# The second batch of a fused attention and FFN kernel takes the order of work of the later batches

## The chip, the cores and the metric

The kernel runs on one core of one Trainium2 chip. The metric is the device time of one execution in microseconds (us): the kernel before takes 320.41 us (median of 3 runs, 319.65 to 321.46). A change counts as faster or slower from 2% on.

Engines are named as in the profile: PE is TensorE (matrix products), PEld its weight loads, DVE VectorE, ACT ScalarE, POOL GpSimd and SP SyncE. A matrix product writes to PSUM, and ACT or DVE read it from there; SBUF is the working memory.

## The reference

Eight batches of attention with eight heads, 576 positions and head dimension 64, with a relative-position bias; then a feed-forward layer (FFN) on the 4608 x 512 result, whose hidden value is the largest of three products.

```python
scores = (1.0 / np.sqrt(D)) * np.matmul(q, k.transpose(0, 1, 3, 2))     # (8, 8, 576, 576)
scores = scores + bias.transpose(2, 0, 1)[None]       # bias_table[bucket(|i - j|)], one table per head
scores = scores - np.max(scores, axis=-1, keepdims=True)
attn = np.exp(scores)
attn = attn / (np.sum(attn, axis=-1, keepdims=True) + 1e-09)
attn_out = np.matmul(attn, v)
x = attn_out.transpose(0, 2, 1, 3).reshape(B * S, H * D)                # 4608 x 512
h = np.maximum(np.maximum(x @ w1, x @ w2), x @ w3)                       # 4608 x 768
out = h @ w_out                                                          # 4608 x 512
```

## The kernel before

The kernel works on pairs of heads: `(b, hp)` is pair `hp` (0 to 3) of batch `b` (0 to 7), so "batch two" is `b == 1`. Scores are made transposed, keys on the partitions. 576 is four tiles of 128 and 64 left over. A pair is done in two halves. Each half has a *visit*, which makes the scores of 256 queries against the 512 main keys: two `sc` tiles in PSUM, four matmuls each, and one exponential each on ACT. The left-over keys give `sct` (one exponential of 576), the left-over queries give `scq` (512 elements in all). DVE multiplies the exponentials with the bias (`times_band`, tile by tile in `t`). One pair later `attend` multiplies them with V into a tile `a`, in two halves, and `quotients` (a reciprocal and a product on DVE) divides by the sums into `x_sb`.

```python
ps_s = ctx.enter_context(tc.tile_pool(name="ps_s", bufs=2, space=bass.MemoryType.PSUM))   # tag "sc": 2 banks each
ps_a = ctx.enter_context(tc.tile_pool(name="ps_a", bufs=2, space=bass.MemoryType.PSUM))   # tag "a"
ps_f = ctx.enter_context(tc.tile_pool(name="ps_f", bufs=2, space=bass.MemoryType.PSUM))   # tag "ff"
...
def visit(qT, kT, e4, c, mid=None, el=None):
    if el is not None:                     # left-over scores inside the visit
        banks = [ps_a.tile([P, KT * 64], F32, tag="a", name="scq") for _ in range(2)]
        turn_left_queries(qT, kT, banks)
        put_left_queries(el, banks)        # two exponentials of 256
    for tt in range(0, KT, 2):
        sc = ps_s.tile([P, 2, 2, QS], F32, tag="sc", name="sc")
        ...                                # four matmuls
        exp(e4[:, tt : tt + 2, :, c * QS : c * QS + QS].rearrange("p t h q -> p h t q"), sc[:])
...
def left_queries(hp, qT, kT, el):          # left-over scores outside the visit
    sc = ps_s.tile([P, 2, CH], F32, tag="sc", name="scq")
    turn_left_queries(qT, kT, [sc[:, par, 0 : KT * 64] for par in range(2)])
    ...                                    # one exponential of 512
...
def second_transposes(made, hp):           # batch two's q and k of a pair are turned by PE
    tp = ps_s.tile([P, 2, 2 * CH], BF16, tag="sc", name="tp")
    ...                                    # ten transposes; dve_copy to qT, act_copy to kT, a main part and a tail each
```

The FFN of earlier tokens fills the gaps of the attention. It is cut into blocks: `f`, `m`, `g` are the products with `w1`, `w2`, `w3`, each worth 4 matmuls of 512 columns (8 of 256 where the chunk has 256 tokens); `o` is an output block of 6. A list of portions holds them, and `fill(rate, *hooks)` takes portions while their sum stays within `rate`. The hooks are the attention's work that stands among the blocks: all of them come before the last block, or earlier if there are more of them than blocks left.

```python
def fill(target, *hooks):
    groups, spent, hooks = [], 0, list(hooks)
    while pending and (not groups or spent + pending[0][0] <= target):
        n, fns = pending.pop(0)
        spent += n
        groups += [fn for fn in fns if fn]
    for j, group in enumerate(groups):
        while hooks and (j == len(groups) - 1 or j > 0 and len(hooks) > len(groups) - 1 - j):
            hooks.pop(0)()
        group()
    for hook in hooks:
        hook()
```

The loop over the pairs, with cuts:

```python
for b, hp in [(b, hp) for b in range(1, B) for hp in range(HP)]:
    ...
    together = b > 1 and (b, hp) != (2, 0)
    rate = 8 if b == 1 or (b, hp) == (2, 0) else 13
    visit(qT, kT, e4, 0)
    ...                                    # a transpose of x_sb of batch 0, where one is left
    quotients = next_late()                # attend of the pair before, first half
    times_band(hp, e4, 0, 0, QS, inorder)
    quotients()
    if b == 1 and hp + 1 < HP:
        spread_packed(hp + 1, nc.vector)   # the next pair's q and k, two copies on DVE
    ...
    def keys():
        left_keys(hp, qT, kT, el, 0, S)    # sct
        if together:
            next_late()()                  # attend of the pair before, second half, and its quotients
    fill(rate, keys, *([lambda: None] if together else []))
    times_bandt(hp, el)

    visit(qT, kT, e4, 1, el=el if together else None)
    ...
    if not together:
        quotients = next_late()            # attend of the pair before, second half
        times_band(hp, e4, 1, 0, QM, inorder)
        quotients()
    if b == 1 and hp + 1 < HP:
        second_transposes(qk[1], hp + 1)
    ...
    fill(rate, bands_2, queries)           # queries: left_queries if not together
    times_band_left(hp, el)
    for half in range(2):
        late.append(lambda b=b, hp=hp, e4=e4, el=el, half=half: attend(b, hp, e4, el, half))
```

Every tag of a PSUM pool is a ring of two: a new tile waits until the tile two before it has been read. The matmuls, the DVE operations of the attention and the copies of the turned q and k keep the order of the program on their engines.

Of the kernel before, what the change touches and what calls it, by code (L numbers as in the profile page):

```python
# [39 lines left out]
def kernel(  # L40
# [19 lines left out]
    HP = H // 2  # L60
    QS = 2 * P
    QM = 2 * QS
# [28 lines left out]
    inorder = tc.keep_in_program_order  # L91
# [4 lines left out]
    def tr(*args):  # L96
        inorder(nc.tensor.transpose(*args))
# [219 lines left out]
    def ffn(t0, nt, last):  # L317
# [77 lines left out]
        f, m, g = ([(DCH, lambda fn=fn, fb=fb: fn(fb)) for fb in range(n_fb)] for fn in (first, second, third))  # L395
        o = [(FCH, lambda j=j: output(j)) for j in range(nt // P)]
        if per == 1:
            portions = [[f[0], m[0]]]
            for fb in range(1, n_fb):
                portions.append([g[fb - 1], f[fb], m[fb]])  # L400
            portions.append([g[-1], (0, None), o[0]])
        else:
            if not t0:
                portions = [[f[0]], [m[0], f[1]], [m[1]], [f[2], m[2]]]
                deferred.append(([[g[0]], g[1:]], [[x] for x in o]))
                o = []
            else:
                portions = [x for gs, _ in deferred for x in gs]
                for fb in range(n_fb):
                    portions += [[f[fb], m[fb]], [g[fb]]]  # L410
                portions += [x for _, os in deferred for x in os] + [[o[0]]]
                o = o[1:]
        if len(o) > 2:
# [3 lines left out]
    pending, rest, stores, deferred, idle_sums = [], [], [], [], []  # L417
# [21 lines left out]
# [13 lines that stand above are left out]
# [55 lines left out]
    def second_transposes(made, hp):  # L507

        hs = slice(2 * hp, 2 * hp + 2)
        tp = ps_s.tile([P, 2, 2 * CH], BF16, tag="sc", name="tp")  # L510
        for j, tl in enumerate((qtail, ktail)):
            for t in range(KT):
                tr(tp[:, j, P * t : P * t + P], batch[1][j][:, t, hs, :].rearrange("p h d -> p (h d)"), ident[:])
            tr(tp[:, j, KT * P : KT * P + P], tl[1][:, hp, :], ident[:])
        main = [
            copy(
                made[j][:, hp, 0 : KT * P].rearrange("c (p t) -> c p t", t=KT),
                tp[:, j, 0 : KT * P].rearrange("c (t p) -> c p t", t=KT),
            )
            for j, copy in enumerate((dve_copy, act_copy))  # L520
        ]
        tail = [
            copy(made[j][:, hp, KT * P :], tp[:, j, KT * P : n])
            for j, (copy, n) in enumerate(((dve_copy, S), (act_copy, (KT + 1) * P)))
        ]
        other_banks([main[1], tail[1]], [main[0], tail[0]])
        other_banks([tail[0]], [main[1]])

    def times_band(hp, e4, t, lo, hi, put=lambda x: x):
        lo, hi = max(lo, P * t - P), min(hi, P * t + 2 * P)  # L530
        if lo < hi:
            c0, c1 = BAND - (hi - P * t + P), BAND - (lo - P * t + P)
            put(nc.vector.tensor_tensor(  # L533
                out=e4[:, t, :, lo:hi], in0=e4[:, t, :, lo:hi],
                in1=hank[:, 2 * hp : 2 * hp + 2, c0:c1][:, :, ::-1], op=ALU.mult,
            ))
# [17 lines left out]
    def visit(qT, kT, e4, c, mid=None, el=None):  # L554

        if el is not None:
            banks = [ps_a.tile([P, KT * 64], F32, tag="a", name="scq") for _ in range(2)]
            turn_left_queries(qT, kT, banks)
            put_left_queries(el, banks)
        for tt in range(0, KT, 2):  # L560
            sc = ps_s.tile([P, 2, 2, QS], F32, tag="sc", name="sc")
            for t in range(2):
                for par in range(2):
                    r = slice(64 * par, 64 * par + 64)
                    mm(
                        sc[:, par, t, :], lhsT=kT[r, P * (tt + t) : P * (tt + t) + P],
                        rhs=qT[r, c * QS : c * QS + QS],
                    )
            exp(e4[:, tt : tt + 2, :, c * QS : c * QS + QS].rearrange("p t h q -> p h t q"), sc[:])
            if tt == 0 and mid:  # L570
                mid()
# [17 lines left out]
    def left_queries(hp, qT, kT, el):  # L589

        sc = ps_s.tile([P, 2, CH], F32, tag="sc", name="scq")
        turn_left_queries(qT, kT, [sc[:, par, 0 : KT * 64] for par in range(2)])
        eq = el[:, S:].rearrange("p (t h q) -> p h t q", t=KT, h=2)
        exp(eq, sc[:, :, 0 : KT * 64].rearrange("p h (t q) -> p h t q", t=KT))
# [75 lines left out]
    def next_late():  # L670
        return late.pop(0)() if late else (lambda: None)
# [9 lines left out]
    qk = [qk_tiles(), qk_tiles()]  # L681
# [45 lines left out]
    for hp in range(HP):  # L727
        qT, kT = (x[:, hp, :] for x in qk[0])
        e4, el = e_tiles()
# [28 lines left out]
    for hp in range(HP):  # L758
        qT, kT = (x[:, hp, :] for x in qk[0])
        e4, el = e_tiles()  # L760
# [20 lines left out]
        quotients = next_late()  # L781
        if hp < 2:
# [5 lines left out]
            quotients = next_late()  # L788
# [24 lines left out]
    for b, hp in [(b, hp) for b in range(1, B) for hp in range(HP)]:  # L813
        if hp == 0:
            x_sb[b] = x_tile()
        qT, kT = (x[:, hp, :] for x in qk[b])
        e4, el = e_tiles()
        together = b > 1 and (b, hp) != (2, 0)
        rate = 8 if b == 1 or (b, hp) == (2, 0) else 13

        visit(qT, kT, e4, 0)
        store_outputs()
        if b == 1:
            if hp == 0:
                crossbar = transposes(2)
            next(crossbar, None)
        elif hp and b + 1 < B:
            if hp == 1:  # L830
                crossbar = transposes(b + 1)
            next(crossbar)
        early()
        if turned:
            turned.pop(0)()
        quotients = next_late()
# [3 lines that stand above are left out]
            spread_packed(hp + 1, nc.vector)  # L840
        if (b, hp) == (1, 1):
            add_ffn(QS, QS)

        def keys():
            left_keys(hp, qT, kT, el, 0, S)
            if together:
                next_late()()

        fill(rate, keys, *([lambda: None] if together else []))
        times_bandt(hp, el)  # L850


        visit(qT, kT, e4, 1, el=el if together else None)
        store_outputs()
        if b == 1 or hp in (1, 2) and b + 1 < B:
            next(crossbar, None)
        early()
        if turned:
            turned.pop(0)()
        if not together:  # L860
            quotients = next_late()
            times_band(hp, e4, 1, 0, QM, inorder)
            quotients()
        if b == 1 and hp + 1 < HP:
            second_transposes(qk[1], hp + 1)
        if hp == 1 and b > 1:
            add_ffn((b - 1) * CH, CH)
        if hp == (2, 2, 0)[min(b, 3) - 1] and b + 1 < B:
            if b == 1:
                load_last_weights(turned_qk[2, 1, 1])  # L870
            load_v(b + 1, 0, H, turned_qk[b + 1, 1, KT - 1] if b < 3 else None)
        if (b, hp) == (2, 0):
            batch[3] = load_tiles()
            load_qk(3, divided[1, HP - 1, 1])
        if hp == 2 and 1 < b < B - 2:
            batch[b + 2] = load_tiles()
            load_qk(b + 2, turned_qk[b + 1, 1, KT - 1])

        def queries():
            if not together:  # L880
                left_queries(hp, qT, kT, el)
            times_band(hp, e4, 3, 0, QM, inorder)

        def bands_2():
            for t in range(1 if together else 2, 3):
                times_band(hp, e4, t, 0, QM, inorder)

        if together:
            idle_sums.append(hp)
        fill(rate, bands_2, queries)  # L890
        idle_sums.clear()
        times_band_left(hp, el)
        for half in range(2):
            late.append(lambda b=b, hp=hp, e4=e4, el=el, half=half: attend(b, hp, e4, el, half))
# [44 lines left out]
```

The softmax here doesn't subtract the row's maximum and nothing guards it: scores larger than these inputs give would overflow.

## Time and profile before

| | busy us | share of the span | instructions |
|---|---|---|---|
| PE | 307.0 | 96% | 3328 |
| DVE | 214.0 | 67% | 535 |
| ACT | 201.3 | 63% | 297 |
| POOL | 108.0 | 34% | 143 |

The span of the profiled execution is 319.7 us, and the granted PE clock is full after the first quarter of the slices. A busy share is a mean over stages with different work, so the stage in question has to be looked at by itself: pairs (1, 0) to (2, 1) lie between 36.2 and 77.1 us of the span. In a timeline, the first number is the start of an instruction (or of a run of equal ones) and the second its length, both in us; the number in brackets is how long its engine had been idle before, and what ended that. Instructions of one engine may overlap a little.

### The profile page before, as it was taken

The page shows a single profiled execution, that of the slowest core. Times are in us where ns is not written, and L with a number is a line of the kernel's source. Part 1 is how long each engine was busy: PE and PEld are TensorE (multiplying, and loading weights), DVE is VectorE, ACT ScalarE, POOL GpSimd, SP SyncE. Part 2 cuts the span into 40 slices and gives each one's busy share as a digit, 9 for nine tenths or more (in the row PEclk, how much of TensorE's full clock was granted, in tenths as well). Part 3 has the DMA queues.
Part 4 walks back from the last instruction along what each step waited for, and adds up shares of the span by engine and source line. Part 5 has one row for each costly group of instructions (what it writes and reads, how often), then busy time and mean ns, then how long its engine had stood idle before and what let it go on. Part 6 is the DMA issues. An engine that isn't in the chain of part 4 may idle for free.

```text
span 319.7 us, 8238 instructions
## 1 busy us (share of the span) xinstructions
PE 307.0 (96%) x3328; PEld 172.1 (54%) x3328; DVE 214.0 (67%) x535; ACT 201.3 (63%) x297; POOL 108.0 (34%) x143
## 2 busy tenths in 40 slices
PE   7768899999999999999999999999999999999995
PEld 2346677775555555555555555555555554444442
DVE  7476678786676666666777667777677675554552
ACT  4958898886677677776777677667776751121221
POOL 8848831349059430852087029500000000000000
PEclk9969999999999999999999999999999999999999
DMA  9999999999999999999999999994042103301103
GB/s 166 198 196 198 180 150 126 135 114 133 206 157 138 127 203 163 84 127 178 190 96 145 163 196 130 157 195 108 2 77 98 36 2 74 133 0 69 64 0 131
DMA packets 163878, 40.34 MB, mean 126 GB/s; under 512 B 153720, under 2 KB 159360, under 8 KB 163840
## 3 DMA queue, kind: packets, MB, share of 16 engines
q0 software_dynamic: 103776, 16.66, 78.0%
q1 hardware_dynamic: 58304, 22.69, 39.1%
q10 hardware_dynamic: 1760, 0.47, 0.6%
q8 instruction: 26, 0.43, 0.6%
q14 instruction: 12, 0.10, 0.1%
HBM read 35.39 MB, written 9.45 MB: 140 GB/s over the span
## 4 chain that ended last, share of the span: by engine, by line
PE 74%; DMA 1%; ACT 1%; issue 0%
PE ps L94 40%; PE pso L94 13%; PE a L94 11%; PE sc L94 7%; PE sct L94 2%; PE scq L94 2%; DMA out_dram<-osb 1%; ACT e L539 0%; ACT osb L388 0%; ACT osb L107 0%
## 5 line engine op out<-in xcount | busy, mean ns | idle before, releaser
L94 PE MATMUL ps<-xT,w_bf 128*128 128x512 bf16 (+1 forms) x720 | 152.2, 358 | 0.6 <-ACT xT L107 0.6
L539 ACT ACTIVATE e<-sc 128x1024 bf16<-128x1024 f32 x128 | 124.5, 1031 | 20.5 <-PE sc L94 17.9
L94 PEld LDWEIGHTS <-w_bf 128*128 128x128 bf16 x720 | 65.4, 98 | 63.4 <-issue 5.8
L533 DVE TENSOR_TENSOR e<-e,hank 128x512 bf16<-128x512 bf16 (+2 forms) x136 | 58.5, 466 | 11.3 <-ACT e L539 9.4
L345 ACT ACTIVATE m<-ps 128x512 bf16<-128x512 f32 x48 | 29.3, 609 | 51.9 <-PE ps L94 51.9
L354 DVE TENSOR_TENSOR m<-ps,m 128x512 bf16<-128x512 f32 x48 | 33.0, 688 | 34.2 <-PE ps L94 34.0
L94 PEld LDWEIGHTS <-kT 64*128 64x128 bf16 (+1 forms) x832 | 30.0, 95 | 38.2 <-issue 25.1
L94 PE MATMUL pso<-wo_bf,hT 128*128 128x512 bf16 (+2 forms) x222 | 50.3, 373 | 0.0
L94 PE MATMUL a<-vx,e 128*128 128x65 bf16 x1024 | 46.4, 195 | 0.0
L360 DVE TENSOR_TENSOR hT<-ps,m 128x512 bf16<-128x512 f32 x48 | 33.0, 688 | 15.9 <-PE ps L94 14.5
L94 PE MATMUL sc<-qT,kT 64*128 64x256 bf16 x512 | 41.0, 273 | 2.8 <-ACT e L539 1.3
L94 PEld LDWEIGHTS <-e 128*128 128x128 bf16 x1024 | 42.1, 99 | 0.8
L139 POOL DMA_DIRECT2D vx<-in_v_dram x32 | 28.5, 911 | 28.8 <-PE scq L94 12.6
L167 POOL DMA_DIRECT2D q_sb<-in_q_dram x24 | 22.0, 918 | 46.2 <-DMA qT<-qtail 26.3
L94 PE MATMUL a<-vt,el 128*128 128x130 bf16 x160 | 36.0, 225 | 0.8 <-DMA vt<-in_v_dram 0.8
L110 DVE COPY osb<-pso 128x512 f32<-128x512 f32 (+1 forms) x33 | 22.6, 686 | 18.0 <-PE pso L94 14.7
L641 DVE TENSOR_TENSOR x_sb<-a,rd 128x256 bf16<-128x256 f32 (+1 forms) x64 | 31.4, 490 | 2.2
L539 ACT ACTIVATE el<-scq 128x256 bf16<-128x256 f32 (+1 forms) x55 | 20.5, 416 | 19.4 <-PE scq L94 19.2
L94 PEld LDWEIGHTS <-hT 128*128 128x128 bf16 x222 | 20.1, 97 | 22.4 <-issue 1.5
L94 PEld LDWEIGHTS <-el 128*128 128x128 bf16 x416 | 24.3, 97 | 10.2 <-issue 5.7
L539 ACT ACTIVATE el<-sct 128x576 bf16<-128x576 f32 (+2 forms) x36 | 21.8, 607 | 5.8 <-PE sct L94 4.5
L167 POOL DMA_DIRECT2D k_sb<-in_k_dram x24 | 22.1, 920 | 1.3 <-DMA w_bf<-in_moe_w_dram 1.2
(71 smaller groups left out, 168.6 us busy)
## 6 DMA issues: line engine op xcount, KB each, us to landing
out_dram<-osb SPq DMA_DIRECT2D x35, 256.0 KB, 3.5
vx<-in_v_dram POOLq DMA_DIRECT2D x32, 128.0 KB, 8.3
q_sb<-in_q_dram POOLq DMA_DIRECT2D x26, 128.0 KB, 5.8
k_sb<-in_k_dram POOLq DMA_DIRECT2D x24, 128.0 KB, 6.7
w_bf<-in_moe_w_dram POOLq DMA_DIRECT2D x3, 768.0 KB, 9.8
xT<-in_k_dram SPq DMA_DIRECT2D x6, 128.0 KB, 4.9
hank<-w_dr SPq DMA_DIRECT2D x2, 384.0 KB, 6.7
wo_bf<-in_moe_w_out_dram POOLq DMA_DIRECT2D x1, 768.0 KB, 7.9
```

Source lines behind the costliest of these rows:

```text
L94: inorder(nc.tensor.matmul(*args, **kw))
L110: return inorder(nc.vector.tensor_copy(out_, in_))
L139: in_turn(b, nc.gpsimd.dma_start(out=dst[:, t, h0:h1, :], in_=x[:, t, h0:h1, :])) for t in range(t0, t1)
L167: loads.append(in_turn(b, nc.gpsimd.dma_start(out=dst[:, t], in_=main_part(src, b)[:, t])))
L345: nc.scalar.activation(out=st[fb]["m0"][:], in_=ps0, func=ACTF.Copy)
L354: inorder(nc.vector.tensor_tensor(out=m[:], in0=ps1, in1=st[fb]["m0"][:], op=ALU.max))
L360: inorder(nc.vector.tensor_tensor(out=block(fb), in0=ps2, in1=other, op=ALU.max))
L533: put(nc.vector.tensor_tensor(out=e4[:, t, :, lo:hi], in0=e4[:, t, :, lo:hi], in1=hank[:, 2 * hp : 2 * hp + 2, c0:c1][:, :, ::-1], op=ALU. ...
L539: nc.scalar.activation(out=out_, in_=in_, func=ACTF.Exp, scale=inv_sqrt_d)
L641: divided[b, hp, half] = inorder(nc.vector.tensor_tensor(out=x_sb[b][:, 2 * half : 2 * half + n, P * hp : P * hp + P].rearrange("p t (h d) ...
```

## The change

Pairs (1, 0) to (2, 0) take the order of work that all later pairs have already. The left-over queries' scores go into the second visit (tag "a" and not "sc", two exponentials and not one), the second half of the pair before is attended in the first half, behind the left-over keys, and its quotients follow at once. The turning of the next pair's q and k, which stood ahead of the second half's FFN, becomes a hook there: behind the first of two blocks, and behind the bands of `t` 1 and 2. The FFN portions of batch 0's second chunk are cut so that a first half gets one block and a second half two, where it was the other way round. Pair (2, 1) gets rate 8 in its first half. It is meant to have the exponentials follow each other more closely, with less waiting for tiles of the tag "sc", and to spread the work more evenly over the halves.

```diff
@@ in ffn(): portions of the second chunk of batch 0
                 for fb in range(n_fb):
-                    portions += [[f[fb], m[fb]], [g[fb]]]
+                    portions += [[f[fb]], [m[fb], g[fb]]]
@@ in the loop over the pairs
-        together = b > 1 and (b, hp) != (2, 0)
         rate = 8 if b == 1 or (b, hp) == (2, 0) else 13
...
         def keys():
             left_keys(hp, qT, kT, el, 0, S)
-            if together:
-                next_late()()
-
-        fill(rate, keys, *([lambda: None] if together else []))
+            next_late()()
+
+        fill(8 if (b, hp) == (2, 1) else rate, keys, lambda: None)
         times_bandt(hp, el)
...
-        visit(qT, kT, e4, 1, el=el if together else None)
+        visit(qT, kT, e4, 1, el=el)
...
-        if not together:
-            quotients = next_late()
-            times_band(hp, e4, 1, 0, QM, inorder)
-            quotients()
-        if b == 1 and hp + 1 < HP:
-            second_transposes(qk[1], hp + 1)
...
         def queries():
-            if not together:
-                left_queries(hp, qT, kT, el)
             times_band(hp, e4, 3, 0, QM, inorder)
 
         def bands_2():
-            for t in range(1 if together else 2, 3):
+            for t in range(1, 3):
                 times_band(hp, e4, t, 0, QM, inorder)
 
-        if together:
-            idle_sums.append(hp)
-        fill(rate, bands_2, queries)
+        idle_sums.append(hp)
+        turn = [lambda: second_transposes(qk[1], hp + 1)] if b == 1 and hp + 1 < HP else []
+        fill(rate, bands_2, *turn, queries)
         idle_sums.clear()
```

`idle_sums` lets the product `f` of a second half write to a tile of the tag "a" instead of "ff".

## The prediction

> **What bounds the kernel now.** I read the page first, then busy time by stretches of 8 us, then the chain of waits, then the timelines of PE, ACT and DVE between 36 and 79 us. The stretches first (columns: stretch; then for PE, PEld, DVE, ACT and POOL busy us and number of instructions; clock; DMA share; GB/s):
>
> ```profile
> 48.00:56.00 8.00, 8.00 (x134) 6.39 (x131) 6.53 (x18) 6.49 (x10) 0.84 (x1) 1.00 1.35 126
> 56.00:64.00 8.00, 7.80 (x123) 6.01 (x120) 6.34 (x18) 7.19 (x11) 2.72 (x4) 1.00 1.06 135
> 64.00:72.00 8.00, 8.00 (x126) 5.96 (x126) 6.46 (x18) 6.94 (x10) 3.76 (x5) 1.00 1.33 113
> ...
> 88.00:96.00 8.00, 8.00 (x95) 4.42 (x94) 5.85 (x14) 5.88 (x9) 4.18 (x6) 1.00 1.06 156
> ```
>
> From about 78 us on PE is the bound: 8.00 of 8 busy, and the chain of waits holds PE pieces end to end. There a second half's scores and its pair's other products cost (starts in the PE timeline) 0.54 for eight `sc`, 0.60 for 18 `a`, 0.24 for `sct`, 0.90 for 27 `a`, 0.13 for eight `scq`, 0.54 for eight `sc`: 2.95 us a pair, and a block of four 512-column products takes 0.86, or 0.216 a unit.
>
> In the changed stretch PE reads as just as busy, but its matmul ends are modelled, and ACT is at 6.5 to 7.2 of 8 and DVE at 6.3 to 6.5: three engines near full, each waiting for the others in turn. So I count PE's need against the clock. Six pairs (1, 0) to (2, 1): 6 x 2.95 = 17.7; FFN units 5 x 12 + 18 = 78, x 0.216 = 16.8; three turnings of ten transposes, 0.56 each = 1.7; three `x_sb` transposes, 0.17 each = 0.5. Sum 36.7. The first `sc` of (1, 0) starts at 36.20 and the first `a` of (2, 2) at 78.21; without waits that `a` would come at 36.20 + 36.7 + 0.53 = 73.4. So PE loses 4.8 us here, 1.5% of the kernel. No work leaves the kernel, and by the start of (2, 2) both orders have done the same 78 units; so 4.8 us is the most that can be gained, and a gain over 2% is as good as excluded.
>
> PE around the last turning:
>
> ```profile
> 55.83 0.38 PE L97 MATMUL tp<-ident,q_sb 128*128 128x128 bf16 x4
> 56.05 0.22 PE L97 MATMUL tp<-ident,qtail 128*128 128x128 bf16 x1
> 56.11 0.39 PE L97 MATMUL tp<-ident,k_sb 128*128 128x128 bf16 x4
> 56.33 0.22 PE L97 MATMUL tp<-ident,ktail 128*128 128x128 bf16 x1
> 56.74 0.29 PE L94 MATMUL scq<-qT,kT 64*128 64x64 bf16 x8 [0.20 <-ACT e L539]
> 56.97 1.05 PE L94 MATMUL ps<-xT,w_bf 128*128 128x256 bf16 x8
> 57.95 0.61 PE L94 MATMUL sc<-qT,kT 64*128 64x256 bf16 x8
> ```
>
> and ACT there and in the next two pairs:
>
> ```profile
> 54.76 1.94 ACT L539 ACTIVATE e<-sc 128x1024 bf16<-128x1024 f32 x2 [0.22 <-PE sc L94]
> 56.59 0.77 ACT L107 ACTIVATE kT<-tp 128x512 bf16<-128x512 bf16 x2
> 57.23 0.61 ACT L539 ACTIVATE el<-scq 128x512 bf16<-128x512 f32 x1
> 58.43 1.94 ACT L539 ACTIVATE e<-sc 128x1024 bf16<-128x1024 f32 x2 [0.59 <-ACT el L539]
> ...
> 69.49 0.60 ACT L539 ACTIVATE el<-scq 128x512 bf16<-128x512 f32 x1
> 70.51 1.94 ACT L539 ACTIVATE e<-sc 128x1024 bf16<-128x1024 f32 x2 [0.42 <-ACT el L539]
> 72.92 0.65 ACT L539 ACTIVATE el<-sct 128x576 bf16<-128x576 f32 x1 [0.47 <-PE sct L94]
> 75.34 0.66 ACT L539 ACTIVATE el<-scq 128x256 bf16<-128x256 f32 x2 [1.76 <-PE scq L94]
> 75.88 3.78 ACT L539 ACTIVATE e<-sc 128x1024 bf16<-128x1024 f32 x4
> ```
>
> The reader should see two kinds of hole on ACT: 0.4 to 0.6 us behind each `scq` exponential, because the next visit's `sc` comes a short `sc` ring later, and 1.76 us in (2, 1), where twelve FFN units stand before `scq`; behind that ACT runs four exponentials without a pause and PE waits for it. These are what the change aims at. And DVE at that turning:
>
> ```profile
> 55.81 0.56 DVE L533 TENSOR_TENSOR e<-e,hank 128x768 bf16<-128x768 bf16 x1 [0.46 <-ACT e L539]
> 56.29 0.19 DVE L640 RECIPROCAL rd<-a 128x6 f32<-128x6 f32 x1
> 56.51 0.56 DVE L641 TENSOR_TENSOR x_sb<-a,rd 128x384 bf16<-128x384 f32 x1
> 56.98 0.78 DVE L110 COPY qT<-tp 128x512 bf16<-128x512 bf16 x2
> 57.68 0.88 DVE L533 TENSOR_TENSOR e<-e,hank 128x768 bf16<-128x768 bf16 x2
> ```
>
> Here the copy to qT comes before the bands that need the second visit's last exponential, and it is done at 57.76, just before the next visit at 57.95.
>
> **What the Trainium skill says.** "ScalarE: Activation LUTs", section "What ACT_TABLE_LOAD costs", gives 186 ns plus 0.833 ns per element for an activation with immediate scale and bias, and an overlap of some 93 ns between two. That is 1039 ns for 1024 and 612 for 512; the trace has 1024 to 1031 and 601. Two of 256 are 2 x 399 - 93, an estimate of 0.71 us; the trace has 0.66 (75.34 above). "TensorE: Matmul & The Clock Gate", section "The mechanism" under packing, says that matmuls start and end in program order; the trace agrees: no `scq` passes an FFN block. "PSUM — Partial Sum Buffer", "Specifications (TRN2)", counts 8 banks of 2 KiB: the three pools take 4 + 2 + 2, so the waits on rings can't be eased by another bank. No view of the trace shows the banks; the sizes in the code do.
>
> **The change part by part.** One pair in the new order, from its first `sc` at 0, in us.
>
> First half, no turning ((1, 3)): the first exponential starts at 0.49 (43.77 to 44.26 in the trace), the second ends at 2.4. PE: `sc` to 0.54, 18 `a` to 1.14, `sct` to 1.38, 27 `a` to 2.28, one block to 3.15. `scq` takes the two tiles of tag "a" that the two attends had, so it waits for the later quotients: reciprocal 0.2 after the last `a` (73.62 to 73.82), 0.79 for reciprocal and product (73.82 to 74.61), so 3.3 us. One block covers 0.87 of that 1.0. ACT: `sct` exponential, the block's copy from 3.4 to 3.9, `scq` to 4.4, then two exponentials to 6.3. PE has its two blocks behind the second visit and reaches the next pair at 5.7; that pair's second `sc` waits for 6.3. So about 5.8 for (1, 3) and 6.0 for (2, 0), against 6.04 each (57.95, 63.99, 70.03). Gain 0.2. The second `scq` exponential adds only 0.06 and lies in ACT's chain.
>
> Pair (2, 1): six units instead of twelve stand before `scq`; the 1.29 us of one output block still cover the quotients. PE needs 2.95 + 3.9 = 6.85 and loses only the start of the second `sc`. I expect the next pair's first `a` 7.7 to 7.8 after its start instead of 8.18. Gain 0.45.
>
> Pairs with a turning ((1, 0), (1, 1), (1, 2)), here (1, 2): two copies of the packed q and k stand on DVE between the two quotients (53.52 to 54.01 in the trace), so `scq` starts at 3.65 and not 3.3. The second visit ends on PE at 4.3, the first block at 5.2. `tp` takes the first `sc`'s tile, whose exponential ends at 5.5: `tp` 5.55 to 6.1, last block to 7.0. On DVE the copy to qT now stands behind the bands of `t` 1 and 2. Band 2 needs the last exponential, which ends at 6.45: band 2 starts at 6.55, 0.48 each, copy main part 0.68 (the 128x512 form), so qT is there at 7.7, and the next `sc` starts at 7.75 instead of 7.0. Before, this pair took 6.87: a loss of 0.9. For (1, 1) the same 7.75 against 7.31: 0.45. For (1, 0), whose first half gets a longer DVE queue (one copy took 0.65) and two more ACT copies, I get 44.5 for the end against 43.77: 0.75. Sum 2.1 lost.
>
> Net: +2.1 - 0.2 - 0.45 = +1.45 us on 320.41, which is 321.9. I take 0.3 off for the rival that I hold likeliest: 321.6.
>
> **The rivals.** First, the gain that was meant: the turning's copies do not matter, because ACT and PE queue enough work. Then the loss of 4.8 us falls to perhaps 3, the three turning pairs take about 6.9 each (21.8 before, 7.57 + 7.31 + 6.87, so 1.1 less), and the sum with the other gains is 318.7. For it speaks that ACT is nearest its limit in these pairs and that the holes of 0.4 to 0.6 are removed; against it, that qT has so little margin already (0.19) and now stands behind one more wait. Second, the wait for the quotients takes the place of the wait on "sc": if DVE is later than I have it, each of six pairs loses 0.3 more, 323.4. For it, DVE is at 6.3 to 6.5 of 8; against, between exponential and quotients I count free time in the first half. Third, nothing: transfers or the later stretch swallow it. In later stretches PE is busy throughout, so a shift in the start of (2, 2) should move the end by just as much; a null would need gains and losses that cancel, 320.4, which is well within reach here.
>
> **Range and chances.** Range 319.2 to 323.2: the lower end is near the first rival, the upper near the second. The bound of 1.5% rules out a faster verdict, and 2% slower would need 6.4 us more, as if all of today's waits came a second time and more. Chances: faster 0.01, same 0.97, slower 0.02.
>
> **What would show it.** Right: in the timeline of the changed kernel the qT copy of the three turnings starts behind a band that waits for ACT's exponential, and the next visit's `sc` starts 0.05 to 0.2 after it, with ACT idle for about 1 us between the kT copy and the next exponential; `scq` starts within 0.1 of the end of an `x_sb` product of 384; pairs (1, 3) and (2, 0) last 5.7 to 6.1; the 1.76 us hole in (2, 1) shrinks, and PE no longer waits in the first visit of (2, 2). From the first `a` of (2, 2) on, both traces should run in parallel. Wrong: turning pairs of 7 us or less, or a qT copy ahead of the bands, would give the first rival; a difference that arises only after 80 us would mean that I looked in the wrong stretch.

## The result and the profile after

| | before | changed | ratio, 95% interval |
|---|---|---|---|
| first comparison | 320.07 us (4 runs) | 323.74 us (4 runs) | 1.0109 [1.0075, 1.0143] |
| second, later | 321.10 us (40 runs) | 323.10 us (21 runs) | 1.0053 [1.0034, 1.0071] |

The changed kernel is slower by 0.5 to 1%, "same" by the 2% rule but clear of noise. 321.6 was predicted, with 323.2 as the upper end; the first comparison lies above it.

The busy time by stretches in the changed kernel (columns as before):

```profile
48.00:56.00 8.00, 7.02 (x108) 5.35 (x106) 6.56 (x19) 5.63 (x9) 0.84 (x1) 1.00 1.23 132
56.00:64.00 8.00, 6.80 (x106) 5.32 (x105) 5.34 (x16) 6.12 (x10) 4.76 (x6) 1.00 1.48 140
64.00:72.00 8.00, 7.84 (x121) 6.10 (x121) 4.67 (x14) 7.07 (x12) 1.35 (x2) 1.00 0.89 68
...
88.00:96.00 8.00, 7.95 (x94) 4.40 (x94) 5.55 (x15) 5.83 (x10) 1.62 (x2) 1.00 0.76 188
```

PE was 8.00, 7.80 and 8.00 in the first three; now it has visible holes, and ACT fell from 6.49 and 7.19 to 5.63 and 6.12 in the first two. From 56 to 64 us PE, ACT and DVE all do less than before, so no engine has become a new bound; the stretches only suggest a longer chain of dependences, and the timelines have to show it. Around the turning behind (1, 2), the counterpart of the one shown of before, PE:

```profile
58.25 0.38 PE L97 MATMUL tp<-ident,q_sb 128*128 128x128 bf16 x4 [0.44 <-ACT e L539]
58.47 0.22 PE L97 MATMUL tp<-ident,qtail 128*128 128x128 bf16 x1
58.53 0.39 PE L97 MATMUL tp<-ident,k_sb 128*128 128x128 bf16 x4
58.75 0.22 PE L97 MATMUL tp<-ident,ktail 128*128 128x128 bf16 x1
58.81 1.04 PE L94 MATMUL ps<-xT,w_bf 128*128 128x256 bf16 x8
60.36 0.61 PE L94 MATMUL sc<-qT,kT 64*128 64x256 bf16 x8 [0.52 <-DVE qT L110]
...
61.92 0.41 PE L94 MATMUL sct<-qT,kT 128*128 128x512 bf16 x2 [0.24 <-ACT e L539]
```

ACT:

```profile
57.16 1.96 ACT L539 ACTIVATE e<-sc 128x1024 bf16<-128x1024 f32 x2
59.01 0.77 ACT L107 ACTIVATE kT<-tp 128x512 bf16<-128x512 bf16 x2
60.84 1.94 ACT L539 ACTIVATE e<-sc 128x1024 bf16<-128x1024 f32 x2 [1.06 <-issue]
62.67 0.66 ACT L539 ACTIVATE el<-sct 128x576 bf16<-128x576 f32 x1
64.13 0.60 ACT L342 ACTIVATE hT<-ps 128x512 bf16<-128x512 f32 x1 [0.81 <-PE ps L94]
```

DVE:

```profile
58.53 1.18 DVE L533 TENSOR_TENSOR e<-e,hank 128x768 bf16<-128x768 bf16 x2
59.62 0.78 DVE L110 COPY qT<-tp 128x512 bf16<-128x512 bf16 x2
60.32 0.41 DVE L533 TENSOR_TENSOR e<-e,hank 128x512 bf16<-128x512 bf16 x1
```

And the chain of waits there (start, length, what):

```profile
57.28 1.84 ACT e L539 x2
59.13 0.02 issue
59.15 0.04 DVE e L533
59.19 0.44 issue
59.62 0.16 DVE qT L110
59.79 1.06 issue
60.84 1.03 ACT e L539
61.88 0.04 issue
61.92 0.41 PE sct L94 x2
```

Read it as a path: the last exponential of a visit, the band that needs it, the copy to qT queued behind that band, the next visit, its first exponential, and then `sct`, which waits for that exponential. (In the kernel before, the chain as the profile follows it back ends at 76.91 us, so it can't be compared here; its timelines can.) `issue` of 1.06 us stands for the rest of the copy's main part (0.68 in all) and the four matmuls ahead of the exponential; the view doesn't name them.

Most comparisons below rest on one measure, the start of the first `sc` of a pair in the PE timeline. "Stage" is from that of (1, 0) to that of (2, 3). What lies ahead of it differs between executions of the same instructions: (1, 0) starts at 36.20 and 34.69 us in two traces of the kernel before, and in the others between 34.15 and 37.40. The stage is steadier: 50.23 and 50.22 in those two, 53.06 and 52.82 in two of the changed kernel. The 0.24 between the last two lies in (1, 0).

| us between first `sc` | (1, 0) | (1, 1) | (1, 2) | (1, 3) | (2, 0) | (2, 1) + (2, 2) | stage |
|---|---|---|---|---|---|---|---|
| before | 7.57 | 7.31 | 6.87 | 6.04 | 6.04 | 16.40 | 50.23 |
| before (second trace) | 7.57 | 7.31 | 6.86 | 6.05 | 6.04 | 16.39 | 50.22 |
| changed | 8.52 | 7.78 | 7.99 | 6.25 | 6.31 | 16.21 | 53.06 |
| changed (second trace) | 8.27 | 7.79 | 7.99 | 6.26 | 6.30 | 16.21 | 52.82 |
| turning first | 8.51 | 7.20 | 7.52 | 6.25 | 6.31 | 16.21 | 52.00 |
| attend first | 8.19 | 7.72 | 7.76 | 5.78 | 6.38 | 16.02 | 51.85 |
| both | 8.49 | 7.12 | 7.81 | 6.18 | 6.17 | 16.02 | 51.79 |
| before, rate 8 in (2, 1) | 7.58 | 7.31 | 6.86 | 6.04 | 6.04 | 16.21 | 50.04 |
| queries behind | 7.46 | 6.81 | 6.61 | 6.02 | 6.01 | 16.02 | 48.93 |
| queries behind, bands first | 7.47 | 7.34 | 7.19 | 6.02 | 6.01 | 16.02 | 50.05 |
| before, turning as hook | 7.57 | 7.56 | 7.20 | 6.04 | 6.04 | 16.39 | 50.80 |
| changed, old portions | 8.45 | 7.79 | 8.25 | 6.15 | 6.85 | 16.51 | 54.00 |
| queries last (second trace) | 7.58 | 6.58 | 6.64 | 6.08 | 6.08 | 15.97 | 48.93 |

In the changed order the length of (1, 0) hangs on a copy. DVE copies the packed q and k of the next pair between the two quotients, and `scq` waits for the second of these. One of the two copies, mostly 0.28 us long, took longer there: 0.74 us in the first trace of the changed kernel, 0.50 in the second, 0.74 in "turning first", 0.41 in "attend first", 0.70 in "both", 0.67 in "changed, old portions". In all six traces (1, 0) less this copy is 7.77 to 7.79 us. So differences of (1, 0) among these six come from the copy, and not from the edits; the last section says what the copy met.

### The profile page after: what moved, and what is told of

Same layout as the page of the kernel before. It is cut to its first block, busy times and chain, and to the rows that moved or that the text cites. A ratio compares the mean times of both kernels' runs of the same rounds, so it can differ in the third digit from the quotient of the medians.

```text
span 322.3 us, 8204 instructions
## 1 busy us (share of the span) xinstructions
PE 306.2 (95%) x3288; PEld 173.2 (54%) x3328; DVE 213.1 (66%) x535; ACT 201.2 (62%) x302; POOL 108.1 (34%) x143
## 4 chain that ended last, share of the span: by engine, by line
PE 79%; ACT 3%; issue 2%; DMA 1%; DVE 1%
PE ps L94 41%; PE pso L94 14%; PE a L94 13%; PE sc L94 7%; ACT e L539 2%; PE sct L94 2%; PE scq L94 2%; DMA out_dram<-osb 1%; DVE e L533 0%; DVE hT L360 0%; ACT kT L107 0%; ACT osb L388 0%; ACT hT L342 0%; ACT el L539 0%; ACT osb L107 0%
## 5 line engine op out<-in xcount | busy, mean ns | idle before, releaser
L94 PE MATMUL ps<-xT,w_bf 128*128 128x512 bf16 (+1 forms) x693 | 148.3, 357 | 2.0 <-ACT xT L107 0.6
L94 PE MATMUL pso<-wo_bf,hT 128*128 128x512 bf16 (+2 forms) x209 | 47.6, 373 | 0.7
```

Source lines behind the costliest of these rows:

```text
L94: inorder(nc.tensor.matmul(*args, **kw))
```

## The experiments

### The turning ahead of the bands

```diff
-        fill(rate, bands_2, *turn, queries)
+        fill(rate, *turn, bands_2, queries)
```

> The changed kernel, with the turning's hook ahead of the bands of t 1 and 2, so that DVE copies qT before it multiplies those bands. Theory A (the copy to qT stands behind a band that waits for the last exponential, and the next visit waits for it): the next visit's first sc comes 0.58 us earlier after (1, 1) and (1, 2), where PE would be done with its last block at 51.78 and 59.78 instead of starting at 52.37 and 60.36; nothing is gained after (1, 0), where the copy to kT on ACT sets the start (44.5). The later bands give back 0.1 to 0.2. Sum -1.0, 322.7 us. Theory B (the loss is in the waits of the first half, sct for the first exponential and scq for the quotients, and the turning is hidden by them): the time moves by less than 0.3 us, 323.5 or more.

Measured: 321.68 us beside 321.15 of before, ratio 1.0023 [0.9998, 1.0047]. The stage is 52.00, 1.06 less than changed: (1, 1) 0.58 and (1, 2) 0.47 shorter, (1, 0) unchanged, as theory A had it. The copy's place behind the bands is one cause, and about 1.1 of the 2.83 us.

### The second attend ahead of the left-over keys

```diff
-            left_keys(hp, qT, kT, el, 0, S)
             next_late()()
+            left_keys(hp, qT, kT, el, 0, S)
```

(It holds for the later batches too, where it changed nothing: (2, 2) takes 8.77 in both traces.)

> The changed kernel, with the second attend ahead of the left-over keys in the first half, so that sct, whose tile is the one of the first sc, is asked for 0.9 us later. Theory B: sct no longer waits 0.24 + 0.2 us for the first exponential; in (1, 3) the left-over queries come 0.4 us earlier, in (1, 1) and (1, 2) nothing is gained since DVE's two copies of packed q and k set the start of scq there, in (2, 0) little. Sum -0.5, 323.2 us, and no wait before sct in the PE timeline. Theory A: that wait is hidden by another one behind it, and the time stays at 323.7 within 0.2.

Measured: 322.12 beside 321.15, ratio 1.0022 [0.9996, 1.0048]; stage 51.85, 1.21 less than changed. No `sct` waits any more. PE in (1, 3):

```profile
62.88 0.41 PE L94 MATMUL a<-vx,el 128*128 128x65 bf16 x8
63.12 0.41 PE L94 MATMUL sct<-qT,kT 128*128 128x512 bf16 x2
63.37 1.04 PE L94 MATMUL ps<-xT,w_bf 128*128 128x256 bf16 x8
64.34 0.29 PE L94 MATMUL scq<-qT,kT 64*128 64x64 bf16 x8
64.46 0.60 PE L94 MATMUL sc<-qT,kT 64*128 64x256 bf16 x8
65.00 1.92 PE L94 MATMUL ps<-xT,w_bf 128*128 128x256 bf16 x16
66.85 0.39 PE L94 MATMUL sc<-qT,kT 64*128 64x256 bf16 x4
```

Everything follows without a wait: 5.78 us for the pair where the changed kernel takes 6.25, a gain of 0.47 for 0.4 expected. (2, 1) and (2, 2) gain 0.19 and (1, 2) gains 0.23. In (1, 2) I had DVE alone in the way; but ACT copies the FFN block's product ahead of the exponential of `scq`, and with `sct` no longer waiting, the block and this copy come 0.40 earlier (3.36 us into the pair and not 3.76), the exponential 0.29 and the turning 0.28 (5.60 and not 5.88). The 0.33 of (1, 0) is luck: the copy there took 0.41 us and not 0.74. Without it the gain is 0.88. Theory B holds as well.

### Both

> Both edits. If A and B each name a wait of its own, the gains add: -1.5, 322.2 us. If they are one chain, the sum is no better than the better of the two, 322.7.

Measured: 321.88 beside 321.15, ratio 1.0026 [1.0008, 1.0044]; stage 51.79, hardly less than with the better edit alone. In (1, 2), 7.81, PE has

```profile
53.77 0.20 PE L94 MATMUL scq<-qT,kT 64*128 64x64 bf16 x1
54.67 0.29 PE L94 MATMUL scq<-qT,kT 64*128 64x64 bf16 x7 [0.70 <-DVE x_sb L641]
```

and DVE ahead of it

```profile
50.25 1.35 DVE L533 TENSOR_TENSOR e<-e,hank 128x768 bf16<-128x768 bf16 x3
51.52 0.68 DVE L360 TENSOR_TENSOR hT<-ps,hT 128x512 bf16<-128x512 f32 x1
...
53.14 0.28 DVE L213 COPY q_sb<-xT 128x512 bf16<-128x512 bf16 x1
53.34 0.59 DVE L213 COPY k_sb<-xT 128x512 bf16<-128x512 bf16 x1
53.85 0.18 DVE L640 RECIPROCAL rd<-a 128x6 f32<-128x6 f32 x1
54.06 0.56 DVE L641 TENSOR_TENSOR x_sb<-a,rd 128x384 bf16<-128x384 f32 x1
```

Two things made `scq` late. The bands that gave way to the copy to qT now run at the start of the next pair and move its quotients by 0.40 us (the first reciprocal starts 2.28 us into the pair, 1.88 in "attend first"). And the copy of k_sb took 0.59 us where it mostly takes 0.29, which adds 0.30. The first cause belongs to the order of work: in (1, 3) it stands alone, the product of the quotients starts 0.40 later, and the pair takes 6.18 for 5.78. The second cause is luck: without it (1, 2) would take about 7.5, an estimate, as with the turning first (7.52). With these copies put at the length that they have in the changed kernel, the stage is 1.06 us shorter by the first edit, 0.88 by the second and about 1.5 by both. So most of the gains add, as the first expectation had it, and some 0.4 is lost to the bands on DVE: part of the first wait turns into the second. The times of the three runs (321.68, 322.12, 321.88) can't tell these apart.

### The kernel before with the even cut of (2, 1) alone

```diff
-        fill(rate, keys, *([lambda: None] if together else []))
+        fill(8 if (b, hp) == (2, 1) else rate, keys, *([lambda: None] if together else []))
```

> The kernel before, with one part of the change alone: rate 8 in the first half of (2, 1), so that one output block stands there and two in the second half. The theory of the prediction: the 1.76 us hole on ACT in (2, 1) shrinks and the four exponentials behind it no longer hold up PE; the first a of (2, 2) comes 0.45 us earlier, 319.6 us. The rival: the block is only moved and PE waits as long elsewhere, 320.1.

Measured: 320.87 beside 321.15, ratio 0.9982 [0.9963, 1.0001]; stage 50.04, 0.19 less. The hole only shrinks, from 1.76 to 1.45 us, as in the changed kernel; PE's wait in the first visit of (2, 2) is gone as expected, but the gain is less than half of 0.45. By the first `a` of (2, 2) it is 0.19 as well (8.18 after the pair's start before, 7.99 here): with the block gone, `sct` stands next to the first `sc` and waits for its tile, 69.70 in this trace against an end of the 18 `a` at about 69.3. The same wait that the prediction overlooked elsewhere.

### A version meant to beat both

```diff
-        fill(8 if (b, hp) == (2, 1) else rate, keys, lambda: None)
+        if behind:              # pairs (1, 0) to (2, 1)
+            fill(8)
+            keys()
+        else:
+            fill(rate, keys, lambda: None)
...
-        visit(qT, kT, e4, 1, el=el)
+        visit(qT, kT, e4, 1, el=None if behind else el)
...
-        idle_sums.append(hp)
+        if not behind:
+            idle_sums.append(hp)
...
-        fill(rate, bands_2, *turn, queries)
+        fill(rate, *turn, *([queries_behind] if behind else []), bands_2, queries)
```

`queries_behind` is the part of `visit` that makes `scq` in two tiles of the tag "a".

> A version meant to beat both kernels, in pairs (1, 0) to (2, 1): the first half's FFN block goes ahead of the left-over keys (it covers sct's wait for the first exponential), the left-over queries go behind the second half's first block in the two tiles of tag a (their wait for the quotients is covered by the second visit and that block), and the turning goes ahead of the bands. Stage from the first sc of (1, 0) to the first sc of (2, 3): 50.2 us before, 53.1 changed. Theory A with B: turning pairs last 6.3 to 6.7, (1, 0) 7.3, (1, 3) and (2, 0) 5.6, stage 47.3, time about 3 us under the kernel before. If the three engines' sums bound the stage and the order of work does not matter, the stage stays near 50.

Measured: 319.97 beside 320.85, ratio 0.9971 [0.9945, 0.9996]: faster than before by 0.3%, just clear of noise, and 0.9 us where 3 were expected; 4.1 us less stage than changed. But the stage is 48.93 and not 47.3: (1, 3) and (2, 0) take 6.0 and not 5.6, although PE waits for no semaphore in them. Their block of eight takes 0.98 us ahead of `sc` or `scq` and 0.87 elsewhere, and `scq` by itself 0.22 where next to `sc` it takes 0.12 to 0.13. PE in (1, 3):

```profile
57.04 1.04 PE L94 MATMUL ps<-xT,w_bf 128*128 128x256 bf16 x8
57.91 0.41 PE L94 MATMUL sct<-qT,kT 128*128 128x512 bf16 x2
...
60.70 0.29 PE L94 MATMUL scq<-qT,kT 64*128 64x64 bf16 x8
60.92 1.05 PE L94 MATMUL ps<-xT,w_bf 128*128 128x256 bf16 x8
61.90 0.61 PE L94 MATMUL sc<-qT,kT 64*128 64x256 bf16 x8
```

### The same with the bands first

```diff
-        fill(rate, *turn, *([queries_behind] if behind else []), bands_2, queries)
+        fill(rate, bands_2, *turn, *([queries_behind] if behind else []), queries)
```

> The same with the bands of t 1 and 2 ahead of the turning, as in the changed kernel. Theory A: the copy to qT again stands behind the band that needs the last exponential, in each of three turning pairs the next visit comes 0.5 to 0.75 us later: stage 1.5 to 2.2 us longer than with the turning first. Theory B: within 0.3 of it.

Measured: 320.54 beside 320.85, ratio 0.9998 [0.9977, 1.0020]; stage 50.05, 1.12 longer: 0.53 in (1, 1), 0.58 in (1, 2), nothing in (1, 0). In (1, 2) DVE and PE show why:

```profile
56.49 1.02 DVE L533 TENSOR_TENSOR e<-e,hank 128x768 bf16<-128x768 bf16 x2
57.43 0.78 DVE L110 COPY qT<-tp 128x512 bf16<-128x512 bf16 x2
```

```profile
56.61 1.05 PE L94 MATMUL ps<-xT,w_bf 128*128 128x256 bf16 x8
58.16 0.61 PE L94 MATMUL sc<-qT,kT 64*128 64x256 bf16 x8 [0.50 <-DVE qT L110]
```

With the turning first the copy starts 5.52 us into the pair (54.79 after 49.27), here 6.46 (57.43 after 50.97). Theory A again, at the size of 0.5 to 0.6 a turning; that (1, 0) is spared, as ACT's copy to kT is later than DVE's there, was not in the 1.5 to 2.2.

### The kernel before with the turning's hook alone

```diff
-        if b == 1 and hp + 1 < HP:
-            second_transposes(qk[1], hp + 1)
...
-        fill(rate, bands_2, queries)
+        turn = [lambda: second_transposes(qk[1], hp + 1)] if b == 1 and hp + 1 < HP else []
+        fill(rate, bands_2, *turn, queries)
```

> The kernel before with one part of the change alone: the turning as a hook behind the bands, nothing else. If the hook's place is harmful by itself: 0.6 us for each of three turnings, stage 52. If it harms only together with the late exponentials of the new order (theory A: before, the last exponential of the visit ends at 56.70, so the band behind it ends before the turning's products are read), at most 0.3 in all, stage 50.2 to 50.6.

Measured: 321.33 beside 320.85, ratio 1.0025 [0.9998, 1.0053]; stage 50.80, 0.57 longer: 0.25 in (1, 1) and 0.33 in (1, 2). Neither expectation: more than 0.3, far less than 1.8. In the old order the last exponential is early, and the band ahead of the copy doesn't wait for it: in (1, 2) the copy starts 6.37 us into the pair and not 5.90, one band's length, and 0.33 of that reaches the next pair. In the new orders the same place costs 0.5 to 0.6, as the band waits there.

### The changed kernel with the old cut of the FFN

```diff
-                    portions += [[f[fb]], [m[fb], g[fb]]]
+                    portions += [[f[fb], m[fb]], [g[fb]]]
```

> The changed kernel with the old cut of the FFN: two blocks in the first half and one in the second, in (1, 2), (1, 3) and (2, 0). The first block then stands ahead of the left-over keys and covers sct's wait, the second covers the quotients, but the turning in (1, 2) finds one block less to hide the wait for the exponential. Theory A with B: (1, 2) 8.1 for 7.99, (1, 3) and (2, 0) 6.1 to 6.2 for 6.25 and 6.31; stage 53.0 within 0.4. The theory that the new cut itself is what costs: stage under 52.

Measured: 323.60 (5 runs) beside 320.85, ratio 1.0088 [1.0053, 1.0123]; stage 54.00, 0.94 longer than changed, so outside the 0.4 that I allowed. (1, 2) and (1, 3) come close to what was expected (8.25, 6.15), (2, 0) takes 6.85. The new cut is not what costs; with the new order it helps. (2, 0) loses because ACT is behind: with a single block after the second visit PE comes to the next visit early and waits for an exponential, 0.52 us at the second `sc` of (2, 0), then 0.23 and 0.52 at the two of (2, 1).

### The left-over queries last, and the changed kernel again

```diff
-        fill(rate, *turn, *([queries_behind] if behind else []), bands_2, queries)
+        fill(rate, *turn, bands_2, queries)
+        if behind:
+            queries_behind()
```

> The version that beat both, with the left-over queries behind the last FFN block of each second half, right ahead of the next visit. In its PE timeline pairs (1, 3) and (2, 0) last 6.0 us with PE never waiting for a semaphore; theory C: PE's need is larger than the prediction's 5.54 a pair because each change from full products to the 64-row products of the scores costs about 0.1 (a block of eight takes 0.97 ahead of sc or scq and 0.87 elsewhere), and scq apart from sc costs 0.22 and not 0.13. One change less a pair: (1, 3) and (2, 0) 5.8, stage 48.9 - 1.0 = 47.9 us. Rival: ACT, which now has the exponentials of scq ahead of the next pair's first one, takes over, and the stage stays at 48.7 to 49.2 or grows.

> The changed kernel itself, beside the kernel before on this chip: stage 53.1 against 50.2, so 2.8 us slower, a ratio of 1.009. If the first result of 3.7 us had more in it than this stage, the ratio stays at 1.011 or more.

Measured: queries last 319.89 beside 321.10, ratio 0.9945 [0.9920, 0.9970], the lowest of all, though the interval overlaps that of "queries behind"; the changed kernel 1.0053 [1.0034, 1.0071], stage 52.82. In its first trace the version with the queries last met something new:

```profile
71.96 0.22 PE L94 MATMUL a<-vt,el 128*128 128x130 bf16 x1 [3.64 <-DMA vt<-in_v_dram]
```

PE waits 3.64 us for the V of batch 2, whose loads POOL issued at 62.0 to 66.8, while the attend of (2, 1) wanted it at 68.3. In the changed kernel's trace POOL issues them at 58.5 and the attend comes at 73.7; in the one of before at 61.3 and 70.6. Behind the wait the granted clock is 0.57 between 73 and 77 us and 1.00 around it, so (2, 1) and (2, 2) take 21.20 us together and not 15.97 as in the later trace. Six of this version's 20 runs took 323.9 to 327.9 us and are left out of the ratio, as are three of the 40 of before; this trace is of one of the six, and whether the others waited for V too isn't shown.

For a trace without that wait, and a second one of before:

> The version with the left-over queries last once more, for a trace in which PE does not wait 3.64 us for V as it did in the first one. Pairs (1, 0) to (2, 0) as there (7.6, 6.6, 6.6, 6.1, 6.1). If the wait was that execution's alone, the stage is 48.5 to 49.0; if this order always gets to V too early, the wait is there again.

> The kernel before once more, for a second trace: if the stage is the same work in every execution, it is 50.2 us again within 0.3, and the rest of the difference between two executions lies ahead of the first sc of (1, 0) or in a wait for a load.

Measured, one run each: 319.22 and 321.09, beside 319.35 of before; single runs settle nothing about the time. No wait for V in either trace; the stages are 48.93 and 50.22. Pairs (1, 3) and (2, 0) of the queries-last version take 6.08 and not 5.8: its rival was right there, ACT takes over and PE waits for the exponential of `sct` in the second visit (in (1, 3) it ends at 58.67 and the second `sc` there starts at 58.73). So this run doesn't carry theory C. The pair (1, 3) of "attend first" and of "queries behind" does: the products of neither wait for a semaphore, and the same products take 5.78 where `scq` stands next to `sc` and 6.02 where it stands alone.

In the second trace of before a later load came late by a little:

```profile
PEld L94 <- DMA kT<-ktail: 1.5, 1, 1.5
PE sct L94 <- DMA kT<-ktail: 1.0, 1, 1.0
```

(the waits after 86 us: total, times, longest). The second trace of "queries last" has such waits for K as well, `sc` 0.5 and `sct` 0.3. In both, 234.4 us follow the stage; in the first trace of before 233.3, and in the two of the changed kernel 233.2.

## Why the prediction was wrong

**Right: the mechanism and the direction.** The copy to qT does start behind a band that waits for the last exponential, the next `sc` starts 0.06 us after the copy's main part (59.62 + 0.68 to 60.36), and ACT is idle 1.06 us. (1, 1) took 7.78 for 7.75 predicted, (1, 2) 7.99 for 7.75; the 0.23 that "attend first" gives back in (1, 2) is the wait of `sct` below, by way of ACT. The turning's position is confirmed in two orders of work, at 0.47 to 0.58 us each for two of three turnings. (1, 0) is 0.95 slower for 0.75, and 0.70 in the second trace; there ACT's copy to kT sets the next `sc`, so the edit that moves DVE's copy gained nothing in it.

**Wrong: "`sct` to 1.38" in the first half.** The step walked PE's work from 18 `a` straight into `sct`. But `sct` has the tag "sc", a ring of two, and takes the tile of the pair's first `sc`, whose exponential ends at 1.5. Before, a block stood between; the change moved it behind. PE in (1, 3) of the kernel before:

```profile
59.10 1.03 PE L94 MATMUL ps<-xT,w_bf 128*128 128x256 bf16 x8
59.98 0.41 PE L94 MATMUL sct<-qT,kT 128*128 128x512 bf16 x2
```

In the changed kernel `sct` starts at 1.56 and not 1.14 (61.92 after 60.36), and the attend, the block and `scq` (3.67 for 3.3) are late by about that. The kernel before already showed it in (1, 1), where no block stands between: `sct` at 45.33, 1.56 us after the first `sc` at 43.77. The wait made (1, 3) and (2, 0), predicted to gain 0.2 together, lose 0.21 and 0.27; taking the wait away gave back 0.47 in (1, 3). The prediction follows the ring for `tp` and for the next visit, and not for `sct`. In (2, 0) the same edit gained nothing, as the second `sc` waits for ACT there.

**Wrong: "2.95 us a pair" and so "PE loses 4.8 us here".** The sum leaves out two costs. Full products take 0.11 us longer ahead of the 64-row products of `sc` or `scq`, twice a pair where `scq` stands next to `sc` and three times where it stands alone; and alone `scq` takes 0.09 more. In the later stretch, from which the durations came, it stands next to `sc`; in the old order of these pairs it stands alone. With these, the 5.54 that I counted for (1, 3) becomes 5.76 and 5.96, for 5.78 measured in "attend first" and 6.02 in "queries behind". The 6.04 of (1, 3) and (2, 0) before was therefore nearly all work in that order; the most that a version here took off it is the 0.26 of "attend first" in (1, 3), where `scq` stands next to `sc` again. A run of matmuls without holes in the timeline should have told me that.

**Mis-sized: (2, 1), 0.45 predicted.** The two pairs (2, 1) and (2, 2) gained 0.19, again for the wait of `sct`: without it, in "attend first", they gained 0.38.

In sum, the stage was to grow by 1.45 and grew by 2.83: 0.44 of the difference from the three turning pairs, 0.68 from (1, 3) and (2, 0), 0.26 from (2, 1). In the second traces it grew by 2.60, 0.25 less in (1, 0).

**The time against the stage.** The first comparison gave 3.67 us, with an interval of 2.4 to 4.6; the second gave 2.0, with 1.1 to 2.3. The stage, 2.83 and 2.60 longer in the traces, lies inside the first interval and above the second. What the rest is I can name only in part: in three traces, the second of before and both of "queries last", PE waits for V or K behind (2, 0), and in the changed kernel's two traces it doesn't. A kernel that waits for loads there would hide part of the changed kernel's loss, but how often it happens isn't shown, and why the two comparisons differ, the first with only four runs each, isn't explained. From (2, 3) on, the first traces of both kernels take the same time, 233.3 and 233.2 us, as predicted.

**The rivals.** "The gain that was meant" fell: the copies do matter. The second, "the wait for the quotients takes the place of the wait on sc", is true in part: it is what the combined edit ran into, and in (1, 0) PE waits 0.40 for `x_sb`. In the other pairs one block nearly covers it. The third, a null, fell too: both intervals lie above 1.

## What to carry to other kernels

When work is moved, go through every tile of every ring in the new order and ask whose reader must be done: a block that seems to be filler may be covering a wait. In an engine that works strictly in order, put the copy that the next stage waits for ahead of work that waits for this stage's end, but look for what then comes later. Take the cost of an engine's work from the stage in question, in the order it has there: a sum of durations from another stage makes full work look like waiting. And before a difference between two traces is put down to an edit, see whether each instruction on the path has its usual length: one long copy made 0.33 us in (1, 0) look like a gain, and another hid a gain of 0.30 in (1, 2).

## What the runs showed of the hardware

A block of eight 256-column products took 0.87 us between full products and 0.98 ahead of the 64-row products of the scores; eight `scq` took 0.12 to 0.13 next to `sc` and 0.22 alone. So a change to the 64-row form cost some 0.1 us in these traces, in a timeline without a visible hole.

The same DVE copy of 512 elements (packed q or k) took 0.27 to 0.29 us in 68 of the 84 cases in the 14 traces and 0.31 to 0.77 in 16. Each of the 16 began 0.26 to 0.63 us after the start of a DMA issue on POOL that was still running, and ended 0.08 to 0.13 us after the end of that issue. In "both", the 0.59 us copy of k_sb from 53.34 to 53.93 goes with

```profile
52.96 0.88 POOL L712 DMA_DIRECT2D wo_bf<-in_moe_w_out_dram  x1 [8.61 <-DMA kT<-k_sb]
```

while the copy of q_sb at 53.14, 0.18 us after the start of the same issue, took 0.28; no copy that began within 0.2 us of an issue's start was long. So the long copies waited for POOL's issue to end, as far as 84 copies show it; no run moved the issues.
